# Fused cross attention and FFN in fp32: the transposes of the states' exponentials by block transposes and DMA, the sum of squares over blocks, and a new order of work

## Chip, cores and metric

The kernel runs on one core of a Trainium2 chip. The metric is the device time of one execution in microseconds. Three executions of the kernel before took 791.08, 791.44 and 792.14 us, median 791.44.

## What is computed

Attention of 8 batches, 8 heads, 512 tokens and 32 states of width 64: the tokens read the states, the states read the tokens, each with its own softmax over scaled scores. The result, 8 x (512 + 32) = 4352 rows of 512, goes through an RMS norm and a gated FFN of width 1536. Everything is fp32.

```python
scores  = x @ state.T / sqrt(64);  a  = softmax(scores);   xread = a  @ state
scores2 = state @ x.T / sqrt(64);  a2 = softmax(scores2);  sread = a2 @ x
rows = concat([xread, sread], axis=2)          # 4352 rows of 512
xn   = rows / sqrt(mean(rows ** 2) + 1e-6) * rms_g
out  = (silu(xn @ w_gate) * (xn @ w_val)) @ w_out
```

## The kernel before

**Stages.** At the start the weights are loaded and batch 0 is computed, beside the attention of batches 0 and 1 (string ORDER, one letter a step). Then the batches 1 to 7 follow, one period each; a period does batch b's FFN and, while b is under 7, the attention of batch b + 1. At the end the FFN of the 256 state rows of all batches is done together (string STATES).

**The FFN of a batch.** Since the token reads are a product of softmax weights and states, the gate and value weights are first multiplied with the batch's own states: `own_weights` (products at L528, copies at L539, both in the function at line 516). One call gives one of six pairs of column blocks, 16 matmuls on small 64x32 tiles of the array (a "group" in the profile is such a run of 16 passes). The hidden layer (`hidden_seven`, products at L674) and the projection (`project_seven`, products at L836) multiply 2x2 blocks with seven products instead of eight, the sums being kept in PSUM banks or formed by VectorE (DVE) and GpSimd (POOL). A product of the projection has two row halves r = 0 and 1, of 12 passes of 128x256 each; the two halves lie in one PSUM bank. When a bank holds a finished partial result, ScalarE (ACT) copies each half to SBUF (L873, names p1, p5, u2, c21), and the products that follow are summed on into the same bank: after p1 and p5 come the sums at L881, and u2 is copied after the product wt,hs, before wo,hb is added into the bank. SBUF sums of h (L888) and stores of the rows (L903, queue of SP) follow.

**The attention of batch b + 1** (`tokens_read` and `states_read`). For batches from 2 on, the scores come from small tiles (L346), in blocks of 32 tokens; DVE transposes blocks of 32x32 (L335, L403). The token reads are products on small tiles (L410), whose squares (ACT, L417) are added by DVE (L420). To get the mean square of each token, four matmuls with a column of ones (L424, eight passes in the profile: an fp32 product is two passes) sum over the partitions; DVE adds 1e-6 (L428), POOL takes the power (L270), four transposes against the identity on TensorE (PE; L277) spread the result over the partitions, and DVE multiplies the softmax weights with it (L434). For the state reads, ACT takes the exponentials of the states' scores (L452, scores copied at L360), PE transposes them, eight 128x128 blocks in two PSUM banks (L459), ACT copies these (L461), and products on small tiles (L471) multiply them with x. DVE divides by the sum (L463, L464, L478), PE transposes once more (L482), DVE copies the result to the state rows (L484).

**Order.** PE, DVE and ACT take their instructions in an order dealt by hand: each letter of PERIOD takes the next step of a generator. Letters h, t, u: products, copies, sums of the hidden layer; p, c, k: products, copies, sums of the projection; v, x: products and copies of own weights; a: `tokens_read(b + 1)`; s: `states_read(b + 1)`; w: the first own weights of batch b + 1. A step is what lies between two `yield`s. POOL and the DMA queues are placed by the framework, which also adds all waits, among them those between the two halves of a PSUM bank: a copy of one half waits for the products before it in the other half, and the products that follow in either half wait for it.

**Buffers.** PSUM pools: aps and vps (attention, own weights) of two banks each, fx of two, fy and fz of one each (FFN). `one` and `two` are SBUF pools of one and two buffers per name.

Of the kernel before, what the change touches and what calls it, by code (L numbers as in the profile page):

```python
# [8 lines left out]
F32 = mybir.dt.float32  # L9
# [3 lines left out]
ALU = mybir.AluOpType  # L13
ACTF = mybir.ActivationFunctionType
AXX = mybir.AxisListType.X
PSUM = bass.MemoryType.PSUM

P = 128
# [10 lines left out]
)  # L29

PERIOD = (
    "hhtvtvhtxhuxhuthhtuhuhtxhhhutuuuhthhuttxahhxhthuuuuuxhavuvhtxhtxhhttuauhxuxhxuut"
    "hhhtuhthutuuhuuuhhauuhtaaauxuhthautuuhhthuhuautaaphuuuapuaaaaacaasapcpaaaaaaaakp"
    "psackaauaacakkpapaakaacpsaskcsssppsasspwswkswxkxxkkpxpxccxss"
)

STATES = (
# [6 lines left out]
def kernel(  # L44
# [20 lines left out]
    nc = tc.nc  # L65
    VE, SE, GE, TE = nc.vector, nc.scalar, nc.gpsimd, nc.tensor
# [75 lines left out]
    GE.memset(bounds[:, 1:2], 255.0 * (1 << 23))  # L142
    rms_g = consts.tile([P, NI], F32, name="rms_g")


    w_d = [scratch.tile([P, NI, 2, 2, P], F32, name="w_d%d" % mp) for mp in range(NM // 2)]
    w_sb = {}
    wo = consts.tile([P, NM, DM], F32, name="wo")
    hb = consts.tile([P, NM, S], F32, name="hb")
# [117 lines left out]
    def mean_root(ss, n):  # L267

        ri = two.tile([P, NC], F32, name="ri")
        GE.tensor_tensor(out=ri[:, 0:n], in0=ss, in1=mhalf[:, 0:n], op=ALU.pow)  # L270
        return ri

    def along_rows(ri, n):

        rp = aps.tile([P, NC, P], F32, name="at")
        for c in range(n):
            TE.transpose(out=rp[:, c, :], in_=ri[:, c:c + 1].to_broadcast([P, P]), identity=ident)  # L277
        return rp.rearrange("p c t -> p (c t)")
# [4 lines left out]
    def scores(b, packed, soft):  # L283

        xb = x_sb[b]
        stT = two.tile([P, 4, Ns], F32, name="stT")
        tp = aps.tile([P, 4, Ns], F32, name="at")
        TE.transpose(out=tp.rearrange("p j n -> p (j n)"),
                     in_=packed.rearrange("p e d -> p (e d)"), identity=ident)
        yield  # L290
        VE.tensor_copy(stT, tp)
        yield "step"

        xT = one.tile([P, 4, NC, P], F32, name="xT", tag="xT")
        for c in range(NC):
            tp = aps.tile([P, 4, P], F32, name="at")
            for j in range(4):
                TE.transpose(out=tp[:, j, :], in_=xb[:, c, P * j:P * j + P], identity=ident)
            yield
            SE.copy(xT[:, :, c, :], tp)  # L300
            yield "step"


        sp = [aps.tile([P, S], F32, name="at") for e in range(2)]
        for j in range(4):
            for e in range(2):
                TE.matmul(out=sp[e][Ns * j:Ns * j + Ns, :], lhsT=stT[D * e:D * e + D, j, :],
                          rhs=xT[D * e:D * e + D, j].rearrange("p c t -> p (c t)"),
                          start=True, stop=True)
        yield  # L310


        sS = read[b] = two.tile([P, 2, NC, P], F32, name="sS")
        eS = soft["e"] = one.tile([P, 2, S // Ns, Ns], F32, name="eS", tag="eS")
        for e in range(2):
            VE.transpose(out=eS[:, e].rearrange("p k n -> p (k n)"), in_=sp[e])
            yield
            SE.copy(sS[:, e].rearrange("p c t -> p (c t)"), sp[e])
            yield "step" if e else None

        soft["st"] = stT
        soft["half"] = lambda e: eS[:, e]
        soft["back"] = lambda e: [(aT_s[b][:, e], eS[:, e].rearrange("p k n -> p (k n)"))]

    def scores_of_blocks(b, packed, soft):
# [30 lines left out]
        for g in (2, 3, 0, 1):  # L356
# [7 lines left out]
                                   eS[:, g].rearrange("p e c n -> p e (c n)"))  # L364
                                  for g in (2 * q, 2 * q + 1)]

    def tokens_read(b):
        packed, soft = rows.pop(b), {}
        yield from (scores if b < 2 else scores_of_blocks)(b, packed, soft)
        half = soft["half"]  # L370
        m1 = two.tile([P, 2, S // Ns], F32, name="m1")
        z1 = two.tile([P, 2, S // Ns], F32, name="z1")

        def along(t, e):
            return t[:, e].unsqueeze(2).to_broadcast([P, S // Ns, Ns])

        for e in range(2):
            VE.reduce_max(out=m1[:, e], in_=half(e), axis=AXX)
            yield
            VE.tensor_tensor(out=half(e), in0=half(e), in1=along(m1, e), op=ALU.subtract)  # L380
            yield
            SE.activation(out=half(e), in_=half(e), func=ACTF.Exp, scale=SCALE)
            yield "step"
        stT_g[b] = two.tile([P, 4, Ns], F32, name="stT_g")
        if b > 1:
            soft["st"] = aps.tile([P, 4, Ns], F32, name="at")
            TE.transpose(out=soft["st"].rearrange("p j n -> p (j n)"),
                         in_=packed.rearrange("p e d -> p (e d)"), identity=ident)
            yield
        VE.tensor_tensor(out=stT_g[b], in0=soft["st"], in1=rms_g.unsqueeze(2).to_broadcast([P, 4, Ns]),  # L390
                         op=ALU.mult)
        yield
        aT_s[b] = two.tile([P, 2, S], F32, name="aT_s")
        for e in range(2):
            VE.reduce_sum(out=z1[:, e], in_=half(e), axis=AXX)
            yield
            VE.tensor_scalar(z1[:, e], z1[:, e], 1e-9, None, op0=ALU.add)
            VE.reciprocal(z1[:, e], z1[:, e])
            yield
            VE.tensor_tensor(out=half(e), in0=half(e), in1=along(z1, e), op=ALU.mult)  # L400
            yield
            for to, blocks in soft["back"](e):
                VE.transpose(out=to, in_=blocks)  # L403
            yield "step"


        reads = [(aps, vps)[j // 2].tile([P, S], F32, name=("at", "pv")[j // 2]) for j in range(4)]
        for j in range(4):
            for e in range(2):
                TE.matmul(out=reads[j][D * e:D * e + D, :],  # L410
                          lhsT=packed[Ns * j:Ns * j + Ns, e, :],
                          rhs=aT_s[b][Ns * j:Ns * j + Ns, e],
                          start=True, stop=True)
        yield
        sq = one.tile([P, 4, S], F32, name="sq", tag="xT")
        for i, j in enumerate((2, 3, 0, 1)):
            SE.activation(out=sq[:, i, :], in_=reads[j], func=ACTF.Square, scale=DM ** -0.5)  # L417
            yield "step" if i == 3 else None
        for i, j in ((0, 1), (2, 3), (0, 2)):
            VE.tensor_tensor(out=sq[:, i, :], in0=sq[:, i, :], in1=sq[:, j, :], op=ALU.add)  # L420
            yield
        sp = aps.tile([P, NC], F32, name="at")
        for c in range(NC):
            TE.matmul(out=sp[:, c:c + 1], lhsT=sq[:, 0, P * c:P * c + P], rhs=ones,  # L424
                      start=True, stop=True)
        yield
        ss = two.tile([P, NC], F32, name="ss")
        VE.tensor_scalar(ss, sp, 1e-6, None, op0=ALU.add)  # L428
        yield "step"
        ri = mean_root(ss, NC)  # L430
        yield
        rp = along_rows(ri, NC)
        yield
        VE.tensor_tensor(out=aT_s[b], in0=aT_s[b],  # L434
                         in1=rp.unsqueeze(1).to_broadcast([P, 2, S]), op=ALU.mult)
        yield "step"

    def states_read(b):

        xb, sS = x_sb.pop(b), read.pop(b)  # L440
        e2 = one.tile([P, 2, NC, P], F32, name="e2")
        s2 = two.tile([P, 2], F32, name="s2")
        m2 = two.tile([P, 2], F32, name="m2")
        z2 = two.tile([P, 2], F32, name="z2")
# [4 lines left out]
        VE.tensor_scalar(s2, m2, -SCALE, None, op0=ALU.mult)  # L449
        yield  # L450
        for e in range(2):
            SE.activation(out=e2[:, e], in_=sS[:, e], func=ACTF.Exp, scale=SCALE,  # L452
                          bias=s2[:, e:e + 1], accum_out=z2[:, e:e + 1])
            yield "step" if e else None
        e2T = one.tile([P, 2, NC, P], F32, name="e2T")
        for e in range(2):
            tp = aps.tile([P, NC, P], F32, name="at")
            for c in range(NC):
                TE.transpose(out=tp[:, c, :], in_=e2[:, e, c, :], identity=ident)  # L459
            yield  # L460
            SE.copy(e2T[:, e], tp)  # L461
            yield "step"
        VE.tensor_scalar(z2, z2, 1e-9, None, op0=ALU.add)  # L463
        VE.reciprocal(z2, z2)  # L464
        yield
# [1 line left out]
        for e in range(2):  # L467
            for c in range(NC):
                for j in range(4):
                    h = 2 * j + e  # L470
                    TE.matmul(out=rp[Ns * j:Ns * j + Ns, e, :],  # L471
                              lhsT=e2T[:, e, c, Ns * j:Ns * j + Ns],
                              rhs=xb[:, c, D * h:D * h + D],
                              start=(c == 0), stop=(c == NC - 1))
        yield
# [567 lines left out]
```

## Time and profile before

| | |
|---|---|
| runs | 791.08, 791.44, 792.14 us |
| profiled execution | 791.18 us, its span 789.0 us |
| TensorE clock granted | 1.00 |
| ACT issues a DMA at L127 | two, at the start, 492 and 601 ns |
| POOL, first power (L270) | 32.94 us, idle for 30.54 us before |
| L403 DVE transpose 128x512 | 707 ns |
| L335 DVE transpose 128x1024 | 1235 ns |
| L395 DVE reduction 128x512 to 128x16 | 662 ns |
| L428 DVE add of 128x4 | 163 ns |
| L461 ACT copy of 128x512 | 580 ns, two a batch |
| L270 POOL power | 1737 ns |
| store of 128 KB / load of 512 KB / x_b, 64 KB / fours, 64 KB | 2.2 / 5.2 / 2.8 / 6.5 us from issue to landing |

The engines are PE, DVE, ACT and POOL; "PEld" is the loading of weights, which overlaps PE. The chain of waits follows the work that ended last back from the end, so that a piece of it is a time in which nothing else set the end. "PE at L424 x8" is eight passes that write the tile named "at". In a table of stretches, busy times stand by engine with the counts of instructions, then the TensorE clock granted, the share of the DMA engines' time that is busy, and the GB/s moved.

### The profile page before, as it was taken

Reading aid. Unit: us, or ns where it says so; the run is one execution under the profiler, and the core shown is the slowest. Engines: PE = TensorE matmul, PEld = TensorE weight load, DVE = VectorE, ACT = ScalarE, POOL = GpSimd, SP = SyncE. Lnnn points to the kernel's source line nnn. Section 1 sums busy time; section 2 is a strip of 40 time slices with the busy share of each in tenths; the row PEclk is TensorE's granted clock in tenths of the full one; section 3 lists DMA queues with packets and bytes.
Section 4 is the critical chain, followed back from the end, with each engine's and each line's share of the span. In section 5 each row is a group of like instructions: output and inputs, shape, how many; then the busy total and the mean of one; then the engine's idle time right before and its main releaser. Section 6 shows DMA issues by size and latency. Waiting matters only on the chain.

```text
span 789.0 us, 13559 instructions
## 1 busy us (share of the span) xinstructions
PE 776.5 (98%) x5478; PEld 603.5 (76%) x5478; DVE 521.5 (66%) x822; ACT 334.4 (42%) x560; POOL 170.9 (22%) x216
## 2 busy tenths in 40 slices
PE   6999999999999999999999999999999999999998
PEld 5643444788877887888878887788788887888996
DVE  4999997688338951897168833895189715781461
ACT  5998864552245323542255224532354225410320
POOL 0100003430244023410433024402341043400000
PEclk9999999999999999999999999999999999999999
DMA  9788865730075005610263008400530034201311
GB/s 286 226 287 298 276 191 167 217 122 1 25 239 181 2 18 181 227 22 17 102 206 121 1 26 257 163 2 15 201 154 7 14 106 149 108 7 34 121 54 27
DMA packets 69277, 95.77 MB, mean 121 GB/s; under 512 B 46432, under 2 KB 54112, under 8 KB 62304
## 3 DMA queue, kind: packets, MB, share of 16 engines
q1 hardware_dynamic: 67040, 94.33, 36.6%
q8 instruction: 43, 0.70, 0.4%
q10 hardware_dynamic: 2176, 0.59, 0.4%
q14 instruction: 18, 0.15, 0.1%
HBM read 79.69 MB, written 15.20 MB: 120 GB/s over the span
## 4 chain that ended last, share of the span: by engine, by line
PE 92%; DVE 5%; DMA 1%; issue 0%; ACT 0%; SPq 0%
PE f L674 37%; PE f L836 35%; PE f L776 5%; PE pv L570 4%; PE at L528 3%; PE pv L528 3%; DVE ex L248 1%; PE at L471 1%; PE at L410 1%; DVE raw L244 1%; PE at L346 1%; PE at L459 1%; PE at L424 1%; DMA raw<-in_moe_w_gate_dram 1%; DVE w_m L253 1%; PE pv L346 1%
## 5 line engine op out<-in xcount | busy, mean ns | idle before, releaser
L836 PE MATMUL f<-wo,hb 128*128 128x256 f32 x540 | 123.4, 380 | 0.2 <-ACT ot L873 0.2
L674 PE MATMUL f<-aT_s,v 128*128 128x256 f32 x504 | 120.6, 382 | 0.0
L836 PEld LDWEIGHTS f<-wo,hb 128*128 128x128 f32 x540 | 101.4, 190 | 13.6 <-ACT ot L873 0.4
L674 PEld LDWEIGHTS f<-aT_s,v 128*128 128x128 f32 x504 | 94.1, 190 | 19.6 <-DVE c L736 5.0
L736 DVE TENSOR_TENSOR g<-g,f 128x512 f32<-128x512 f32 (+1 forms) x96 | 61.8, 653 | 68.4 <-PE f L674 63.9
L674 PE MATMUL f<-aT_t,vs 128*128 128x256 f32 x336 | 87.1, 381 | 0.0
L270 POOL TENSOR_TENSOR ri<-ss,mhalf 128x4 f32<-128x4 f32 x8 | 13.5, 1692 | 320.4 <-DVE s L449 210.9
L727 ACT ACTIVATE hb<-g 128x1024 f32<-128x1024 f32 (+1 forms) x48 | 48.2, 1004 | 79.3 <-DVE g L736 79.3
L836 PE MATMUL f<-wt,hs 128*128 128x256 f32 x360 | 81.0, 381 | 0.0
L836 PEld LDWEIGHTS f<-wt,hs 128*128 128x128 f32 x360 | 67.3, 190 | 14.1 <-issue 5.1
L674 PEld LDWEIGHTS f<-aT_t,vs 128*128 128x128 f32 x336 | 63.2, 190 | 15.0 <-issue 5.9
L873 ACT COPY ot<-f 128x256 f32<-128x256 f32 x60 | 21.4, 373 | 123.0 <-PE f L836 123.0
L554 POOL TENSOR_TENSOR vs<-v 128x256 f32<-128x256 f32 x42 | 31.3, 746 | 164.2 <-ACT v L539 164.1
L739 DVE SCALAR_TENSOR_TENSOR hb<-hb,g 128x1024 f32<-128x1024 f32 x42 | 53.2, 1266 | 4.6 <-ACT hb L727 4.6
L725 ACT COPY g<-f 128x512 f32<-128x512 f32 (+1 forms) x48 | 26.9, 561 | 55.8 <-PE f L674 55.8
L776 PE MATMUL f<-wo,hb 128*128 128x512 f32 x96 | 44.7, 600 | 0.0
L557 POOL TENSOR_TENSOR vs<-v,vs 128x256 f32<-128x256 f32 x42 | 44.4, 1057 | 0.0
L570 PE MATMUL pv<-aT_s,v 128*128 128x512 f32 x96 | 43.7, 594 | 0.2 <-DVE aT_s L434 0.2
L674 PE MATMUL f<-aT_s,vs 128*128 128x256 f32 x168 | 43.1, 379 | 0.0
L674 PE MATMUL f<-aT_t,v 128*128 128x256 f32 x168 | 43.1, 379 | 0.0
L836 PE MATMUL f<-wo,hs 128*128 128x256 f32 x180 | 41.1, 379 | 0.0
L836 PEld LDWEIGHTS f<-wt,hb 128*128 128x128 f32 x180 | 33.7, 190 | 9.4 <-DVE ot L881 5.0
(144 smaller groups left out, 1277.0 us busy)
## 6 DMA issues: line engine op xcount, KB each, us to landing
w_m<-w_d SPq DMA_DIRECT2D x48, 1024.0 KB, 6.5
out_dram<-ot SPq DMA_DIRECT2D x56, 128.0 KB, 2.2
raw<-in_moe_w_val_dram SPq DMA_DIRECT2D x6, 1024.0 KB, 5.5
raw<-in_moe_w_out_dram SPq DMA_DIRECT2D x6, 1024.0 KB, 8.6
x_b<-in_x_dram SPq DMA_DIRECT2D x96, 64.0 KB, 2.8
w_d<-w_m SPq DMA_DIRECT2D x6, 1024.0 KB, 4.9
raw<-in_moe_w_gate_dram SPq DMA_DIRECT2D x5, 1024.0 KB, 7.1
x_b<-in_x_dram SPq DMA_DIRECT2D x6, 256.0 KB, 6.8
```

What stands on the lines that cost most here:

```text
L528: TE.matmul(out=pv[e][Ns * j:Ns * j + Ns, :], lhsT=stT_g[b][D * e:D * e + D, j, :], rhs=w[D * e:D * e + D, j].rearrange("p m k f -> p (m k ...
L554: GE.tensor_tensor(out=vs[:, 0], in0=a21, in1=a22, op=ALU.add)
L557: GE.tensor_tensor(out=vs[:, 2], in0=a12, in1=vs[:, 1], op=ALU.subtract)
L570: TE.matmul(out=to[0], lhsT=lhs(i, k), rhs=r, start=(i == 0), stop=(i == len(rhs) - 1))
L674: TE.matmul(out=ps[:, i, 0:half], lhsT=l[:, i, :], rhs=r, start=(start and i == 0 and k == 0), stop=(k == len(lhs) - 1), skip_group_check= ...
L725: SE.copy(gates(q)[1], q["x"][:, :, 0:half])
L727: SE.activation(out=hb[:, 2 * mp:2 * mp + 2, 0:n].rearrange("p m (c t) -> p m c t", c=2), in_=q["g"][:, :, :, 0:half], func=ACTF.Silu if s ...
L736: VE.tensor_tensor(out=to, in0=to, in1=q[ps][:, :, 0:half], op=ALU.add)
L739: VE.scalar_tensor_tensor(out=h, in0=h, scalar=1.0, op0=ALU.add, op1=ALU.mult, in1=q["g"].rearrange("p m c t -> p m (c t)"))
L776: TE.matmul(out=banks[r], lhsT=hb[:, m, P * r:P * r + P], rhs=wo[:, m, :], start=(m == 0), stop=(m == NM - 1))
L836: TE.matmul(out=banks[name][:, r, :], lhsT=lhs(k)[:, P * r:P * r + P], rhs=rhs(k), start=(start and r == 0 and k == 0), stop=(k == HM - 1) ...
L873: SE.copy(to, banks[name][:, r, :])
```

## The change

For batches 2 to 7 the exponentials of the states' scores are written by ACT in another layout (L493), transposed in 32x32 blocks by one DVE instruction (L512), written to DRAM by a DMA that ACT issues (L515, 512 KB), and read back in four DMAs of 128 KB each (L519), also issued by ACT. That replaces eight PE transposes and two ACT copies per batch. The small product L530 (old L471) takes its weights from the new layout.

For the same batches the sum of squares over the partitions is done by blocks (`rms_on_blocks`): DVE transposes 32x32 blocks (L395), sums each over its free axis (L398), one matmul with a fixed 128x128 matrix of 32x32 identities (`groups`, built by sixteen POOL operations at the start) adds the partition groups (L401, 128x128 by 128x16), and four DVE additions of 32 partitions each (L406) replace one of 128. `stT` moves from the pool `two` to `one`. Batches 0 and 1 keep the old way (`rms_on_array`).

The string PERIOD is dealt anew. ORDER and STATES stay as they are. In the new order the own weights' groups stand mostly alone between FFN products, and the two row halves of wo,hb in the projection (L896, old L836), with ACT's copy of the second half of u2 (L933, old L873) between them, follow one another on PE with nothing between. The lines of the old functions move down by 8 at first and by 38 to 60 from `tokens_read` on: L674 becomes L734, L836 L896, L528 L588, L410 L458, L277 L285, L420 L468, L881 L941, L888 L948.

```diff
--- before.py
+++ after.py
@@
 PERIOD = (
-    "hhtvtvhtxhuxhuthhtuhuhtxhhhutuuuhthhuttxahhxhthuuuuuxhavuvhtxhtxhhttuauhxuxhxuut"
-    "hhhtuhthutuuhuuuhhauuhtaaauxuhthautuuhhthuhuautaaphuuuapuaaaaacaasapcpaaaaaaaakp"
-    "psackaauaacakkpapaakaacpsaskcsssppsasspwswkswxkxxkkpxpxccxss"
+    "hhvttvhtxhuhuhxuxthuhtthuhhuthxhuxhuuhtthahuuthtuhuvhxutauhhtxutxhhuuhxhthvuuthh"
+    "axttxuhuuhthuhxhuuuutahhuahutthtuuhuahuuhupaatuauhauupucaaaasaaaaaaapsacksppsasc"
+    "aappacaacakpkakaupsaasaacaaspsakksaaaspkkpasawwsspxwxxckpxsxksxc"
 )
...
+    groups = consts.tile([P, 4, Ns], F32, name="groups")
+    for i in range(4):
+        GE.tensor_copy(groups[:, i], ident[:, 0:Ns])
+        for j in range(1, 4):
+            GE.tensor_tensor(out=groups[:, i], in0=groups[:, i],
+                             in1=ident[:, Ns * j:Ns * j + Ns], op=ALU.add)
...
+    e_d = [scratch.tile([4, Ns, 4, 8 * Ns], F32, name="e_d%d" % k) for k in range(2)]
...
+    def rms_on_array(b, sq):
...
+    def rms_on_blocks(b, sq):
+        n = S // Ns
+        VE.transpose(out=sq[:, 1, :], in_=sq[:, 0, :])
+        yield
+        part = one.tile([P, n], F32, name="part")
+        VE.reduce_sum(out=part, in_=sq[:, 1, :].rearrange("p (k f) -> p k f", f=Ns), axis=AXX)
+        yield
+        sp = aps.tile([P, n], F32, name="at")
+        TE.matmul(out=sp, lhsT=groups.rearrange("p i t -> p (i t)"), rhs=part,
+                  start=True, stop=True)
+        yield
+        ss = two.tile([P, NC], F32, name="ss")
+        for g in range(4):
+            VE.tensor_scalar(ss[Ns * g:Ns * g + Ns], sp[Ns * g:Ns * g + Ns, g::4], 1e-6, None,
+                             op0=ALU.add)
+        yield "step"
+        ri = mean_root(ss, NC)
+        yield
+        rp = along_rows(ri, NC)
+        yield
+        return rp
...
     def tokens_read(b):
...
-        sp = aps.tile([P, NC], F32, name="at")
-        for c in range(NC):
-            TE.matmul(out=sp[:, c:c + 1], lhsT=sq[:, 0, P * c:P * c + P], rhs=ones,
-                      start=True, stop=True)
-        yield
-        ss = two.tile([P, NC], F32, name="ss")
-        VE.tensor_scalar(ss, sp, 1e-6, None, op0=ALU.add)
-        yield "step"
-        ri = mean_root(ss, NC)
-        yield
-        rp = along_rows(ri, NC)
-        yield
+        rp = yield from (rms_on_array if b < 2 else rms_on_blocks)(b, sq)
...
     def states_read(b):
...
-        e2 = one.tile([P, 2, NC, P], F32, name="e2")
+        e2 = one.tile([P, 4, 2, NC, Ns], F32, name="e2")
...
         for e in range(2):
-            SE.activation(out=e2[:, e], in_=sS[:, e], func=ACTF.Exp, scale=SCALE,
+            to = e2[:, :, e].rearrange("p g c t -> p c g t")
+            if b < 2:
+                to = exps[:, e]
+            SE.activation(out=to, in_=sS[:, e].rearrange("p c (g t) -> p c g t", t=Ns)
+                          if b > 1 else sS[:, e], func=ACTF.Exp, scale=SCALE,
                           bias=s2[:, e:e + 1], accum_out=z2[:, e:e + 1])
...
-        for e in range(2):
-            tp = aps.tile([P, NC, P], F32, name="at")
-            for c in range(NC):
-                TE.transpose(out=tp[:, c, :], in_=e2[:, e, c, :], identity=ident)
-            yield
-            SE.copy(e2T[:, e], tp)
-            yield "step"
+        e2T = one.tile([P, 4, 2, NC, Ns], F32, name="e2T")
+        if b < 2:
...
+        else:
+            eB = one.tile([P, 4, 2, NC, Ns], F32, name="eB", tag="eS")
+            VE.transpose(out=eB.rearrange("p g e c n -> p (g e c n)"),
+                         in_=e2.rearrange("p g e c t -> p (g e c t)"))
+            yield
+            nc.scalar.dma_start(out=e_d[b % 2].rearrange("j t g f -> (j t) (g f)"),
+                                in_=eB.rearrange("p g e c n -> p (g e c n)"))
+            yield
+            for g in range(4):
+                nc.scalar.dma_start(out=e2T[Ns * g:Ns * g + Ns].rearrange("t j e c n -> t j (e c n)"),
+                                    in_=e_d[b % 2][:, :, g].rearrange("j t f -> t j f"))
+                yield
```

More of the change, by code (lines that the diff above doesn't have):

```diff
@@ L285, in scores @@
         xb = x_sb[b]
-        stT = two.tile([P, 4, Ns], F32, name="stT")
+        stT = one.tile([P, 4, Ns], F32, name="stT")
         tp = aps.tile([P, 4, Ns], F32, name="at")
@@ L365, in scores_of_blocks @@
                                   for g in (2 * q, 2 * q + 1)]
+    def rms_on_array(b, sq):
+        sp = aps.tile([P, NC], F32, name="at")
+        for c in range(NC):
+            TE.matmul(out=sp[:, c:c + 1], lhsT=sq[:, 0, P * c:P * c + P], rhs=ones,
+                      start=True, stop=True)
+        yield
+        ss = two.tile([P, NC], F32, name="ss")
+        VE.tensor_scalar(ss, sp, 1e-6, None, op0=ALU.add)
+        yield "step"
[13 more added lines that the diff above has]
+        TE.matmul(out=sp, lhsT=groups.rearrange("p i t -> p (i t)"), rhs=part,
+                  start=True, stop=True)
+        yield
+        ss = two.tile([P, NC], F32, name="ss")
+        for g in range(4):
+            VE.tensor_scalar(ss[Ns * g:Ns * g + Ns], sp[Ns * g:Ns * g + Ns, g::4], 1e-6, None,
+                             op0=ALU.add)
+        yield "step"
+        ri = mean_root(ss, NC)
+        yield
+        rp = along_rows(ri, NC)
+        yield
+        return rp
     def tokens_read(b):
@@ L440, in states_read @@
         xb, sS = x_sb.pop(b), read.pop(b)
-        e2 = one.tile([P, 2, NC, P], F32, name="e2")
+        e2 = one.tile([P, 4, 2, NC, Ns], F32, name="e2")
+        exps = e2.rearrange("p g e c t -> p (g e c t)").rearrange("p (e c s) -> p e c s", e=2, s=P)
         s2 = two.tile([P, 2], F32, name="s2")
@@ L451, in states_read @@
         for e in range(2):
-            SE.activation(out=e2[:, e], in_=sS[:, e], func=ACTF.Exp, scale=SCALE,
+            to = e2[:, :, e].rearrange("p g c t -> p c g t")
[3 more added lines that the diff above has]
+                          if b > 1 else sS[:, e], func=ACTF.Exp, scale=SCALE,
                           bias=s2[:, e:e + 1], accum_out=z2[:, e:e + 1])
             yield "step" if e else None
-        e2T = one.tile([P, 2, NC, P], F32, name="e2T")
-        for e in range(2):
-            tp = aps.tile([P, NC, P], F32, name="at")
-            for c in range(NC):
-                TE.transpose(out=tp[:, c, :], in_=e2[:, e, c, :], identity=ident)
-            yield
-            SE.copy(e2T[:, e], tp)
-            yield "step"
+        e2T = one.tile([P, 4, 2, NC, Ns], F32, name="e2T")
+        if b < 2:
+            flat = e2T.rearrange("p j e c n -> p (j e c n)").rearrange("p (e c s) -> p e c s", e=2, s=P)
+            for e in range(2):
+                tp = aps.tile([P, NC, P], F32, name="at")
+                for c in range(NC):
+                    TE.transpose(out=tp[:, c, :], in_=exps[:, e, c, :], identity=ident)
+                yield
+                SE.copy(flat[:, e], tp)
+                yield "step"
+        else:
+            eB = one.tile([P, 4, 2, NC, Ns], F32, name="eB", tag="eS")
+            VE.transpose(out=eB.rearrange("p g e c n -> p (g e c n)"),
+                         in_=e2.rearrange("p g e c t -> p (g e c t)"))
+            yield
+            nc.scalar.dma_start(out=e_d[b % 2].rearrange("j t g f -> (j t) (g f)"),
+                                in_=eB.rearrange("p g e c n -> p (g e c n)"))
+            yield
+            for g in range(4):
+                nc.scalar.dma_start(out=e2T[Ns * g:Ns * g + Ns].rearrange("t j e c n -> t j (e c n)"),
+                                    in_=e_d[b % 2][:, :, g].rearrange("j t f -> t j f"))
+                yield
         VE.tensor_scalar(z2, z2, 1e-9, None, op0=ALU.add)
@@ L471, in states_read @@
                     TE.matmul(out=rp[Ns * j:Ns * j + Ns, e, :],
-                              lhsT=e2T[:, e, c, Ns * j:Ns * j + Ns],
+                              lhsT=(e2T[:, j, e, c, :] if b > 1 else
+                                    flat[:, e, c, Ns * j:Ns * j + Ns]),
                               rhs=xb[:, c, D * h:D * h + D],
```

## The prediction

> **What bounds it.** I read first the busy shares, then the chain that ended last by engine:
>
> ```profile
> PE 776.5 (98%) x5478; PEld 603.5 (76%) x5478; DVE 521.5 (66%) x822; ACT 334.4 (42%) x560; POOL 170.9 (22%) x216
> ...
> PE 92%; DVE 5%; DMA 1%; issue 0%; ACT 0%; SPq 0%
> ```
>
> PE alone sets the time. In the chain the first products of batches 2 to 7 (pieces "L674 x8") begin at 223.04, 308.52, 394.00, 479.48, 564.96 and 650.43 us, 85.48 apart: six equal periods (batches 1 to 6, with batch b+1's attention inside), then batch 7's without attention and the states' rows. The changed work lies at a period's end; its chain:
>
> ```profile
> 287.55 0.79 PE at L424 x8
> 288.34 2.70 PE f L836 x12
> 291.04 0.44 PE at L277 x4
> 291.47 0.44 PE at L459 x4
> 291.91 5.18 PE f L836 x24
> 297.09 0.44 PE at L459 x4
> 297.53 2.59 PE f L836 x12
> 300.12 1.03 PE at L471 x64
> 301.15 1.02 PE pv L528 x16
> 302.17 0.86 PE at L528 x16
> 303.03 5.38 PE f L836 x24
> ```
>
> Nothing but PE, end to end: what PE no longer does is saved in full, every wait of PE costs in full, and other engines matter only where they come late. A 128x256 pass takes 5.18/24 = 0.216 us here. The group after L424 takes 2.70 instead of 2.59, and the one after the small tiles of L528 5.38 instead of 5.18: such pieces cost their neighbour too.
>
> **Part 1, off PE in each of six periods.** L424's eight passes: 0.79 + (2.70 - 2.59) = 0.90. L459's eight transposes: 2 x 0.44 = 0.88. Together 1.78.
>
> **Part 2, onto PE.** L401, one 128x128 by 128x16 product, two passes. No row has it; L424 (128x1) takes 0.90/8 = 0.11 a pass, a transpose (128x128) 0.11. I take 0.22; ends 0.11 and 0.38.
>
> **Part 3, the own weights' groups dealt apart.** The old order puts L528's groups in pairs or behind L471: five runs of small-tile work a period ({L528 x2}, {L528 x2}, L346, L410, {L471, L528 x2}). The new one has seven ({L588 x2}, L588, L588, L354, L458, {L588, L530}, L588). In batch 0 the chain shows both kinds:
>
> ```profile
> 99.95 1.02 PE at L528 x16
> 100.97 1.91 PE f L776 x4
> ...
> 109.75 1.72 PE f L776 x4
> ```
>
> A group alone costs 1.02 and makes the next full group 1.91 instead of 1.72, so about 1.21; the second of a pair costs 0.86. Each split adds 0.36 (ends 0.31 and 0.43, by the chain's 1.09 for another lone one): 0.72 a period. [...]
>
> **Part 4, waits for half a bank.** A copy of one half of a PSUM bank waits for the products already queued into the other half, and the products that refill its half wait for the copy. Before, this pair is covered:
>
> ```profile
> 291.07 0.37 ACT L873 COPY ot<-f 128x256 f32<-128x256 f32 x1 [1.55 <-PE f L836]
> 291.31 0.60 PE L459 MATMUL at<-ident,e 128*128 128x128 f32 x4
> 291.75 2.75 PE L836 MATMUL f<-wo,hb 128*128 128x256 f32 x12
> ```
>
> The copy starts as wo,hb's first half ends (291.04) and is done at 291.44, while PE does eight transposes to 291.91. In the new order wo,hb's second half (L896) follows the first directly on PE, and ACT's copy (L933) between them still waits for the first. The u2 copy of the other row lies beside the reads L458 (1.05 and the 0.2 behind it), one c21 copy beside a lone L588 (1.02): both longer than a copy with its ends (0.44). So one uncovered wait a period. It stands uncovered in the old kernel's last period, where no attention lies:
>
> ```profile
> 716.91 0.02 issue
> 716.93 0.38 ACT ot L873
> 717.31 0.04 issue
> 717.36 13.22 PE f L836 x60
> ```
>
> That is 0.44; 13.22 less 60 x 0.216 is 0.26 more for draining and restarting: 0.70. Ends 0.63 and 0.82. Behind the waiting product stand L401, wo,hs, L285 and all later PE work, so it is paid in full.
>
> **Part 5, DVE and ACT.** DVE gets the transposes L512 (128x1024, 1.24 by L335's row) and L395 (0.70, by L403's 707 ns for the same shape), the sum L398 (0.67, by L395 of the old kernel), and four 0.16 us adds instead of one: 3.1 us a period, beside 54.8 busy of 86. ACT loses two copies of 0.58 and gains five DMA issues (its old issues, at L127, took 0.49 to 0.60). What matters is lateness. Counting from the start of L458's products (0): squares end at 1.10 + 1.97 = 3.1. The three L468 adds, L395 and L398 end at 3.1 + 3 x 0.69 + 0.70 + 0.67 = 6.5 if L512 is done before the squares. L401 is due at 1.17 + 3 x 2.59 + 0.70 = 9.6: slack 3.1. Behind L401: four adds 0.64, POOL's power 1.74, so ri by 12.3; L285 is due at 9.64 + 0.22 + 5.18 = 15.0: slack 2.7. The DMA issue waits for L512, which follows exponentials before the reads; on ACT the bank copy of part 4 stands behind it, due at 1.17 + 2 x 2.59 = 6.4, so L512 has some 3 us. The rows for the window say there is room: columns are us, then busy of PE, PEld, DVE, ACT, POOL, clock, DMA share, GB/s.
>
> ```profile
> 281.00:288.00 7.00, 7.00 (x48) 5.51 (x47) 3.54 (x7) 2.70 (x6) 0.00 (x0) 1.00 0.16 47
> 287.00:297.00 10.00, 10.00 (x56) 8.92 (x55) 2.98 (x7) 2.75 (x7) 4.58 (x5) 1.00 0.04 15
> ```
>
> I cost all of it at nothing; one microsecond late is 6 us in all. [...]
>
> **Part 6, the round trip through DRAM.** The write (512 KB) and four reads (128 KB, 1 KB pieces) lie between eB and L530. L530 is due at 1.17 + 3 x 2.59 + 0.70 + 0.22 + 2 x 2.59 + 0.44 + 1.02 = 16.5, the write is issued by 3.1: 13.4, less 5 x 0.55 for issues, leaves 10.65 for both landings. By rows: a 512 KB load 5.2; 128 KB stores 2.2, and 64 KB loads in small pieces 2.8 (x_b) or 6.5 (fours). So 7.4 to 11.7; I take 5.2 + 2.8 = 8.0, hidden, DMA share being 0.04 there. Reads queue ahead of ACT's copies of the lone L588's bank, which come at 16.5: no loss.
>
> **Start and end.** POOL gets sixteen small operations at the start; its first power for a batch is 33 us in, and it idles before: nothing. In batch 7's period one more group is split (0.36) and one more copy stands almost uncovered (0.06): 0.42 added.
>
> **Sum.** Per period -1.78 + 0.22 + 0.72 + 0.70 = -0.14; six: -0.84; with 0.42: -0.4. The profiled execution took 791.18 (span 789.0 and 2.2 around it), 0.26 below the median of 791.44: 790.8 against it, 791.0 against the median. At all upper ends (+0.16 + 0.14 + 0.12 a period) it is +2.2: 793.6; at the lower ones, -2.2: 789.2.
>
> **Rivals.** (a) Faster, the bank wait isn't on the path: the framework's dependency may not tie the second half to that copy, or PE's queue hides it. Then six times -0.84, plus 0.42: -4.6, 786.8. For it: the six steady periods of before show no ACT piece; against it: the row at 716.91, and that there PE had other work in between.
> (b) Slower, the round trip is late. Place: L530 waits for the last read; price 6 us per us; it decides from 10.65 us for both landings. With the worst rows (5.2 + 6.5) it is 1.05 late: +6.3, 797.3. For it: 1 KB pieces, four reads on one queue behind one wait; against it: the idle DMA.
> (c) Slower, DVE's longer chain is late at L401 or the write's issue at the u2 copy: slack about 3, so it would take two 1.2 us operations queued ahead; 1 us late gives 797.
> (d) It doesn't do what it says: part 1's passes only stood where PE would have waited anyway. Part 4 has this already: 0.70 of 1.78.
>
> **Chances.** The sum 0.62 with its own range 789.2 to 793.6, of which 0.08 lies faster by over 0.2% (1.6 us, what a measurement here can tell from no change), 0.06 slower and 0.48 within. (a) 0.20, faster. (b) 0.10, (c) and the like 0.08, slower. Faster 0.28, same 0.48, slower 0.24. The range takes the sum and (a), 0.82: 786.6 to 793.6.
>
> **What will show it.** Periods 0.14 shorter (85.34). Right: an ACT piece of 0.38 at L933 between two L896 pieces in every period's chain; a lone L588 at 1.02 with its next group 0.2 longer; L401 about 0.2; no DMA or DVE piece near L530 and L401. Wrong: no ACT piece (a), "DMA e2T" before L530 (b), DVE before L401 or L512 before a late copy (c). A changed clock or POOL on the chain would be outside all of it.

## The result and the profile after

The changed kernel takes 791.60 us (median of 4 runs, 791.00 to 791.67), the kernel before 791.79 on the same chip: a ratio of 0.9997, 95% interval 0.9979 to 1.0014, no change that this measurement can tell. Forecast was a fall of 0.4. The changed kernel's profiled execution took 791.00, its span 789.2.

The page of the changed kernel, busy shares, then the chain by engine:

```profile
PE 774.4 (98%) x5394; PEld 593.0 (75%) x5394; DVE 545.2 (69%) x858; ACT 327.6 (42%) x548; POOL 173.8 (22%) x232
...
PE 94%; DVE 2%; ACT 2%; issue 0%; DMA 0%; SPq 0%
```

PE issues 84 passes fewer, DVE is busy 24 us longer (18.6, six times 3.1, were forecast), and PE is still the bound. In the chain the first products of batches 2 to 7 (pieces "L734 x8") begin at 223.31, 308.69, 394.07, 479.44, 564.83 and 650.20: a period of 85.38, against 85.48 before and 85.34 forecast. The end of such a period, in the changed kernel's chain (start, us, what):

```profile
285.39 5.39 PE f L896 x24
290.79 0.02 issue
290.81 0.38 ACT ot L933
291.19 0.04 issue
291.24 2.86 PE f L896 x12
294.09 0.13 PE at L401 x2
294.22 5.28 PE f L896 x24
299.50 0.44 PE at L285 x4
299.93 1.02 PE pv L588 x16
300.95 1.03 PE at L530 x64
301.98 2.79 PE f L896 x12
304.77 1.02 PE at L588 x16
305.79 2.79 PE f L896 x12
```

Every term of the sum can be read here. There are no passes with ones and no exponentials' transposes. ACT's copy stands on the path between wo,hb's halves: 0.44 of waiting, and a group of 2.86 instead of 2.59 behind it, 0.71 together. L401 takes 0.13, and the group behind it 5.28 instead of 5.18: 0.23. The last five rows hold the same products as the old rows from L471 to the 5.38 group, in 8.65 us (their sum) against 8.29: the second L588 stands alone and takes 1.02 instead of 0.86, and both groups of L896 now follow small tiles and take 2.79 instead of 2.59, where before only one paid this; 0.36 in all. The two DMA steps do not appear in the chain. Their rows:

```profile
e_d<-eB ACTq DMA_DIRECT2D x6, 512.0 KB, 2.9
e2T<-e_d ACTq DMA_DIRECT2D x24, 128.0 KB, 3.0
```

In the period shown eB is written from 285.67 on; the reads are issued from 290.89 to 292.65, since the first stands behind the copy of 290.81 on ACT; the last lands near 295.3. L530 begins at 300.95, so more than 5 us are left.

### The profile page after: what moved, and what is told of

Its sections match the earlier page's. It is cut to its first block, busy times and chain, and to the rows that moved or that the text cites. A ratio compares the mean times of both kernels' runs of the same rounds, so it can differ in the third digit from the quotient of the medians.

```text
span 789.2 us, 13508 instructions
## 1 busy us (share of the span) xinstructions
PE 774.4 (98%) x5394; PEld 593.0 (75%) x5394; DVE 545.2 (69%) x858; ACT 327.6 (42%) x548; POOL 173.8 (22%) x232
## 4 chain that ended last, share of the span: by engine, by line
PE 94%; DVE 2%; ACT 2%; issue 0%; DMA 0%; SPq 0%
PE f L734 38%; PE f L896 35%; PE f L836 5%; PE pv L630 4%; PE at L588 3%; PE pv L588 3%; PE at L530 1%; PE at L458 1%; PE at L354 1%; PE f L987 1%; PE pv L354 1%; PE at L285 0%; DMA rows<-in_state_dram 0%; PE at L306 0%; ACT ex L225 0%
## 5 line engine op out<-in xcount | busy, mean ns | idle before, releaser
L896 PE MATMUL f<-wo,hb 128*128 128x256 f32 x540 | 123.5, 381 | 3.0 <-ACT ot L933 3.0
L734 PE MATMUL f<-aT_s,v 128*128 128x256 f32 x504 | 122.5, 384 | 0.0
L896 PEld LDWEIGHTS f<-wo,hb 128*128 128x128 f32 x540 | 102.1, 190 | 18.9 <-ACT ot L933 5.6
L734 PEld LDWEIGHTS f<-aT_s,v 128*128 128x128 f32 x504 | 93.7, 190 | 24.9 <-issue 12.2
L734 PE MATMUL f<-aT_t,vs 128*128 128x256 f32 x336 | 87.1, 382 | 0.0
L933 ACT COPY ot<-f 128x256 f32<-128x256 f32 x60 | 21.3, 368 | 157.5 <-PE f L896 157.5
L896 PE MATMUL f<-wt,hs 128*128 128x256 f32 x360 | 82.2, 382 | 0.0
L278 POOL TENSOR_TENSOR ri<-ss,mhalf 128x4 f32<-128x4 f32 x8 | 9.3, 1157 | 330.5 <-DVE ss L406 223.8
L896 PEld LDWEIGHTS f<-wt,hs 128*128 128x128 f32 x360 | 67.3, 190 | 13.9 <-ACT ot L933 4.9
L734 PEld LDWEIGHTS f<-aT_t,vs 128*128 128x128 f32 x336 | 63.3, 190 | 14.8 <-issue 5.9
L599 ACT COPY v<-pv 128x512 f32<-128x512 f32 x42 | 23.7, 598 | 60.0 <-PE pv L588 60.0
L836 PE MATMUL f<-wo,hb 128*128 128x512 f32 x96 | 44.7, 600 | 0.0
L734 PE MATMUL f<-aT_t,v 128*128 128x256 f32 x168 | 43.1, 379 | 0.0
L734 PE MATMUL f<-aT_s,vs 128*128 128x256 f32 x168 | 43.1, 379 | 0.0
L896 PE MATMUL f<-wt,hb 128*128 128x256 f32 x180 | 42.6, 387 | 0.0
```

Of the source, the lines that this page charges most:

```text
L599: SE.copy(v[:, e].rearrange("p m k f -> p (m k f)"), pv[e])
L734: TE.matmul(out=ps[:, i, 0:half], lhsT=l[:, i, :], rhs=r, start=(start and i == 0 and k == 0), stop=(k == len(lhs) - 1), skip_group_check= ...
L836: TE.matmul(out=banks[r], lhsT=hb[:, m, P * r:P * r + P], rhs=wo[:, m, :], start=(m == 0), stop=(m == NM - 1))
L896: TE.matmul(out=banks[name][:, r, :], lhsT=lhs(k)[:, P * r:P * r + P], rhs=rhs(k), start=(start and r == 0 and k == 0), stop=(k == HM - 1) ...
```

## The experiments

A copy's wait is called covered where PE has other work while ACT copies. All kernels but one are the changed kernel with an edit; their periods are the distances between equal pieces in the chain of batches 1 to 6 (four or five of five agree within 0.02 us). The chain's place at the start of the first period differed from 139.2 to 140.4 us over the thirteen profiles of this study, whose opening part hardly differs, so sums are judged by periods, and medians beside them. Each ratio is to runs of the kernel before that were taken beside it (their medians are 791.79 to 791.91).

| kernel | period, us | median, us | ratio to before (95%) |
|---|---|---|---|
| before | 85.48 | 791.79 | |
| changed | 85.38 | 791.60 | 0.9997 (0.9979 to 1.0014) |
| e1_cover | 85.34 | 790.80 | 0.9985 (0.9976 to 0.9995) |
| e8_cover_hs | 84.77 | 787.11 | 0.9938 (0.9924 to 0.9953) |
| e2_pairs | 84.84 | 788.39 | 0.9957 (0.9942 to 0.9972) |
| e3_both | 84.81 | 786.65 | 0.9938 (0.9922 to 0.9955) |
| e9_all | 84.23 | 783.74 | 0.9901 (0.9886 to 0.9916) |
| e4_pe_exps_between | 85.52 | 792.32 | 1.0010 (1.0001 to 1.0019) |
| e5_array_rms_between | 85.32 | 791.46 | 0.9994 (0.9985 to 1.0004) |
| e6_before_blocks_rms | 85.32 | 790.54 | 0.9985 (0.9975 to 0.9994) |
| e10_all_array_rms | 84.79 | 786.43 | 0.9937 (0.9922 to 0.9952) |
| e11_all_pe_exps | 85.05 | 788.72 | 0.9960 (0.9946 to 0.9974) |
| e7_late_trip | 87.8 to 94.9 | 818.56 (one run) | |

**The copy's wait, covered: e1_cover.** The edit is in PERIOD alone, its last line: both u2 copies (c) and then the reads (a) follow wt,hs's second half (p).

```diff
-    "aappacaacakpkakaupsaasaacaaspsakksaaaspkkpasawwsspxwxxckpxsxksxc"
+    "aappacaakpccakakaupsaasaaaaspsakksaaaspkkpasawwsspxwxxckpxsxksxc"
```

> The changed kernel with one thing moved: the token reads (L458) stand behind both halves of wt,hs, and both u2 copies stand ahead of them, so that the copies lie beside the reads and wo,hb's second half waits for no copy. My theory (the uncovered wait costs 0.70 a period and is paid in full): a period of 85.38 becomes 84.68, and no ACT piece is left between two L896 pieces in the chain of batches 1 to 6; in batch 7's period, which has no reads, both copies stand uncovered together, 0.37 more; in all -3.8, about 787.8. Rival 1 (the wait only takes the place of another, such as L401 or L285 coming late, since the reads now begin 2.6 us later): the period stays near 85.4 and the time near 791.6, with DVE or POOL before L401 or L285. Rival 2 (only the 0.44 of the ACT piece is lost, the longer group behind it isn't part of it): a period of 84.94, about 789.4.

Measured: 85.34, only 0.04 less. The ACT piece is gone, and another engine stands in its place. Chain of e1_cover:

```profile
292.56 0.69 DVE part L398
293.24 0.88 DVE hs L948
294.12 0.04 issue
294.17 5.45 PE f L896 x24
```

So rival 1 held, though not at L401 or L285: DVE takes its work in the order dealt, and hs, which wo,hs needs, stood behind the squares' sums and the two new operations L395 and L398. Ahead of these the chain also holds ACT's squares, with the issue of the write (L515, 0.35) between them. What the change adds to DVE and ACT was free in the changed order, where PE waits for the copy; in this one it isn't. Batch 7's period became 0.4 shorter, where 0.37 longer was expected; my term for it was wrong, since the states' first products stand between there.

**The same with hs ahead: e8_cover_hs.** Two letters k (hs, L948) move ahead of the squares' sums.

```diff
-    "aappacaakpccakakaupsaasaaaaspsakksaaaspkkpasawwsspxwxxckpxsxksxc"
+    "aappacaakpccakakaupskkaasaaaaspsasaaaspkkpasawwsspxwxxckpxsxksxc"
```

> The kernel e1_cover with one more thing moved: the two subtractions hs (L948) stand on DVE ahead of the squares' sums, not behind the transpose and the sum over blocks (L395, L398). In e1_cover the copies were covered, but the chain went through the squares, L395, L398 and L948 to the product wo,hs, and gave a period of 85.34. Theory (the wait of 0.70 is real, and e1_cover only put DVE's longer queue in its place): with hs ahead the period is 84.68, 0.66 below e1_cover, and PE has no piece but its own between reads and L285; about 786.8. Rival (whatever is late is late for the squares themselves, which begin 2.6 us later: then L401 or L285 waits next): 84.9 to 85.3 with DVE or POOL pieces ahead of L401 or L285; 788 to 790.5.

Measured: 84.77, 0.61 under the changed kernel and 787.11. From the reads to L285 its chain holds PE alone, with one piece that is longer than before; that row of the chain, then the row of the timeline for its weights' load (in brackets the idle time before):

```profile
292.27 0.24 PE at L401 x2
```

```profile
292.12 0.30 PEld L401 LDWEIGHTS at<-part,groups 128*128 128x128 f32 x2 [0.25 <-issue]
```

L401 takes 0.24 instead of 0.13: L398 begins at 291.31 and lasts 0.69, so `part` is there at 292.00, and the load of L401's weights begins at 292.12, 0.15 before the 24 passes ahead of it end (292.27); in the changed kernel it begins at 293.71, 0.38 before that end. L401's new delay takes 0.11, so the covered wait gave 0.72. The price of 0.70 in the prediction is shown to be real and paid in full, once DVE is in time.

**The groups put together: e2_pairs.** One letter v moves next to another, and L530 stands ahead of both groups of the next batch.

```diff
-    "hhvttvhtxhuhuhxuxthuhtthuhhuthxhuxhuuhtthahuuthtuhuvhxutauhhtxutxhhuuhxhthvuuthh"
+    "hhvttvhtxhuhuhxuxthuhtthuhhuthxhuxhuuhtthahuuthtuhuvvhxutauhhtxutxhhuuhxhthuuthh"
...
-    "aappacaacakpkakaupsaasaacaaspsakksaaaspkkpasawwsspxwxxckpxsxksxc"
+    "aappacaacakpkakaupsaasaacaaspsakksaaaspkkpasawswswpxxxkpcxsxksxc"
```

> The changed kernel with the two groups of own weights that the new order splits off put back: L588 of the fourth and fifth pair of column blocks together, and L530 directly ahead of both groups of the next batch (with the c21 copy behind both halves of wt,hb, as in the kernel before). My theory (0.36 for each lone group): the period falls by 0.72 from 85.38 to 84.66, batch 7's period by 0.36; in all -4.7, about 786.9. Rival (the small tiles cost the same alone or in a pair, and the longer group behind a lone one is an effect of how ends are modelled): no change, 791.6.

Measured: 84.84, 0.54 less instead of 0.72; 788.39. Around L530 the rows give 8.29 instead of 8.65, all of the 0.36. In the hidden layer they give 30.08 instead of 30.27, only 0.19: the 60 passes behind the pair take 13.33, where its own last period, without attention, takes 13.15 for the same. The timeline of e2_pairs has the reason:

```profile
337.44 0.73 PEld L734 LDWEIGHTS f<-aT_t,v 128*128 128x128 f32 x4 [0.32 <-DVE c L796]
```

The lone group had stood just ahead of a product that waits for DVE to empty its bank. Half of its 0.36 was cover. The small tiles' price is real (the rival falls), and it too depends on what stands behind.

**Both at once: e3_both, then e9_all with hs ahead.** e3_both has the letters of e1_cover and e2_pairs, e9_all those of e8_cover_hs and e2_pairs.

> The edits of the two kernels before together: the copies of u2 covered by the reads, and no own weights' group split off. My theory (the terms add): the period falls by 1.42 to 83.96, batch 7's period gains 0.36 and loses 0.37; in all -8.5, about 783.1. Rival (with 1.4 us less of PE in a period something else comes late: the powers before L285, the copies of the own weights, or the return of the exponentials before L530): a period between 84.0 and 85.0 with DVE, POOL or DMA pieces in its chain, 784 to 789.

Measured: 84.81, with L398 and L948 of DVE in the chain as in e1_cover; the rival held. The groups took 0.53 off e1_cover's period, as they took 0.54 off the changed kernel's; what is missing is the covered wait, for the reason found in e1_cover.

> The three edits of e1_cover, e8_cover_hs and e2_pairs together: copies of u2 beside the reads, hs ahead of the squares' sums on DVE, no own weights' group split off. Theory (what was measured adds up: 0.61 for the covered wait with hs ahead, 0.54 for the groups): a period of 84.23, batch 7's period 0.4 shorter; about 783.6. Rival (e3_both gave only 84.81 because a period of this work cannot go under it, some other engine's round being the limit): 84.6 to 84.8, 785 to 786.7, with DVE, POOL or DMA pieces in the period's chain.

Measured: 84.23 and 783.74, as the terms add up. This is 1.0% under the kernel before (0.9901, 0.9886 to 0.9916), with nothing changed in the new code but the order.

**One part undone, at the place of the wait: e4_pe_exps_between, e5_array_rms_between.** Both take the old way for all batches; the old passes stand between wo,hb's halves. In e4_pe_exps_between (`states_read`; each test of b, and six letters s become four):

```diff
-    "aappacaacakpkakaupsaasaacaaspsakksaaaspkkpasawwsspxwxxckpxsxksxc"
+    "aappacaacakpkakaupaaaacsssaapsakkaaapkkpasawwsspxwxxckpxsxksxc"
...
-        if b < 2:
+        if b < B:
```

In e5_array_rms_between (`tokens_read`, and two letters a fewer):

```diff
-        rp = yield from (rms_on_array if b < 2 else rms_on_blocks)(b, sq)
+        rp = yield from (rms_on_array if b < B else rms_on_blocks)(b, sq)
```

> The changed kernel with the exponentials of the states' scores transposed on PE again for all batches (the way of batches 0 and 1, no DMA), the eight transposes put between the two halves of wo,hb, where ACT's copy is waited for. My theory: they cost 0.88 a period and hide the wait of 0.70, so the period grows by 0.18 to 85.56; in all +1.1, about 792.7, with no ACT piece in the chain. Rival 1 (the transposes cost their 0.88 wherever they stand, since the wait isn't on the path): 86.26, 796.9. Rival 2 (the round trip through DRAM holds the changed kernel up somewhere): the period falls below 85.38, the time below 791.

> The changed kernel with the mean square taken on PE again for all batches (eight passes with a column of ones, no L395 and L398), put between the two halves of wo,hb where ACT's copy is waited for. My theory: 0.90 comes back, 0.23 of L401 goes, and the wait of 0.70 is covered: the period falls by 0.03 to 85.35, 791.4, with no ACT piece in the chain of batches 1 to 6. Rival 1 (the wait is not what these passes cover): +0.67, 86.05, 795.6. Rival 2 (DVE's added work holds the changed kernel up where the chain doesn't show it): below 85.2.

Measured: 85.52 and 85.32, each within 0.04 of the theory and 0.7 from the first rival. Two rows of e4's chain tell it:

```profile
291.36 0.87 PE at L504 x8
292.23 2.59 PE f L896 x12
```

The eight transposes take 0.87, and behind them the group is 2.59 long again, with no ACT piece. Moving them to DVE and DMA saved 0.14 of 0.88 at this place, and taking the mean square off PE lost 0.06: each set free the same wait of 0.71.

**One part undone where nothing waits: e10_all_array_rms, e11_all_pe_exps.** The same two edits in e9_all's order.

> e9_all with the mean square on PE again for all batches (eight passes with the column of ones where L401 stood, no L395 and L398). Theory (where no copy is waited for, the eight passes cost PE all they take): 0.90 less 0.23 back, a period 0.67 above e9_all's, 84.90; 4.0 above it. Rival (these passes would be hidden again behind some other wait): within 0.2 of e9_all's period.

> e9_all with the exponentials of the states' scores transposed on PE again for all batches, four transposes behind L401 and four between the halves of wo,hs, no DMA. Theory (where no copy is waited for, eight transposes cost 0.88): a period 0.88 above e9_all's, 85.11; 5.3 above it. Rival (they cover something, as between the halves of wo,hb): within 0.3 of e9_all's period.

Measured: +0.56 and +0.82 a period, 786.43 and 788.72. The first is 0.90 less 0.34, because L401 costs 0.24 and 0.10 in e9_all; in the second the transposes take 0.48 and 0.44, and the 0.10 that L401 adds to its neighbour is gone, since they stand between. Here the saved passes are saved. No run has the old way of both in this order; if the two differences add, its period would be 85.61 (an estimate), no better than the 85.48 of the kernel before: the order would then pay only with the new code.

**The sum over blocks in the old order: e6_before_blocks_rms.** The kernel before with `rms_on_blocks` for batches 2 to 7 and two letters a more (L873 of its rows is L836 of before).

```diff
-    "psackaauaacakkpapaakaacpsaskcsssppsasspwswkswxkxxkkpxpxccxss"
+    "psackaauaacakkpapaaaakaacpsaskcsssppsasspwswkswxkxxkkpxpxccxss"
```

> The kernel before, in its own order, with the sum of squares over blocks alone (L395, L398, L401 in place of the eight passes; the exponentials' transposes stay on PE). My theory (the eight passes covered the copy of u2's first half): 0.79 and 0.11 go, the copy's 0.44 with the 0.27 behind it comes, L401 lies inside it; the period falls by 0.19 from 85.48 to 85.29, in all -1.1, about 790.7, with an ACT piece of 0.38 ahead of wo,hb in every period. Rival 1 (saved passes are saved): -0.67, 84.81, 787.8. Rival 2 (DVE's longer queue puts hs off ahead of wo,hs, as in e1_cover): above 85.4, 791 to 793, with DVE ahead of wo,hs.

Measured: 85.32 and 790.54, near the 85.29 and 790.7 of the theory and far from rival 1. But the chain names another engine:

```profile
287.67 0.70 DVE part L398
...
288.50 0.37 PE at L401 x2
```

L401's operands come at 288.37, and the copy of u2's first half runs from 288.38 to 288.75. Both are late by nearly the same time. The run shows that 0.5 of the saved 0.67 is lost at this place; which of the two would lose it alone, it doesn't tell.

**The round trip made late: e7_late_trip.** L512, the write and the reads move behind L406.

```diff
-    "aappacaacakpkakaupsaasaacaaspsakksaaaspkkpasawwsspxwxxckpxsxksxc"
+    "aappacaacakpkakaupaaaacaapakkaaasssssspkkpasawwsspxwxxckpxsxksxc"
```

> The changed kernel with the transpose of the states' exponentials (L512) moved behind the additions L406 on DVE, and write and reads behind it. By the rows of the changed kernel eB is then ready at 296.2 on the profile's clock, the write lands 2.9 later, the last of four reads is issued 1.3 later and lands 3.0 later: 303.4, while L530 is due at 300.95. My theory (the trip is hidden in the changed kernel by 5 us, and every us late is one in each of six periods): L530 waits 2.4 us for a DMA, a period of 87.8, in all +14.7, about 806. Rival (the trip overlaps whatever PE has queued, or the engine's queue runs ahead): 791.6.

Measured: 818.56, 27 us more instead of 14.7. The five distances between the first products of batches 2 to 7 are 94.9, 89.4, 89.2, 87.8 and 89.2. Chain in the second of them:

```profile
398.79 3.11 DMA e2T<-e_d
...
402.25 1.55 PE at L530 x64
403.80 3.96 PE f L896 x12
```

The lone L588 ends at 399.43, and L530 begins at 402.25. One product of 0.43 fits between, so 2.4 us are lost, as expected. The rest is the clock: it is at 0.50 from 402.7 to 406.1, so that L530 takes 1.55 instead of 1.03 and the next twelve passes 3.96 instead of 2.79, 1.7 more. The fourth distance shows the wait by itself: L530 begins at 580.82, as late as elsewhere, the clock stays at 1.00, and 87.8 is just 2.4 over the changed kernel. In the longest one the write takes 4.64 to land, and the weights' load of 1 MB is issued at 304.78, with the reads: the last of these takes 5.79, and the DMA engines are busy 0.78 of 306 to 312. The trip is hidden in the changed kernel because it is early, and it is not small.

## Why the prediction was right

**What bounds it** held: PE throughout, six equal periods.

**Parts 1 and 2** held. 0.90 and 0.88 a period leave PE (0.79 and 0.11 in e10_all_array_rms, 0.87 in e4_pe_exps_between); L401 is 0.23 against 0.22.

**Part 3** held: 0.36 and 0.37 for the two split groups. That 0.17 of one price is cover for a bank's wait was not in the prediction. The rows and e2_pairs fit 0.36 us for each separate run of small tiles; what in TensorE takes this time they do not show.

**Part 4** held to 0.01: 0.44 and 0.27 at the place named, and e8_cover_hs got 0.72 back. That the 0.27 goes to draining and restarting, as the prediction puts it, is not shown. Rival (a) is refuted by the ACT piece in the chain.

**Part 5** held for the changed kernel: L398 ends at 290.50 and L401 is due at 294.09, 3.6 us of room where 3.1 were counted. But "I cost all of it at nothing" is true of this order only; e1_cover and e3_both, where the copy's wait is covered, run into exactly these operations. The product that then waits is wo,hs, for hs behind L398 on DVE; the prediction looks at L401, L285 and the copy, and not at hs. The price given with it, 6 us in all for a microsecond late, holds only while the clock does: for 2.4 us of lateness the distances of e7_late_trip grew by 2.4 once, by 3.8 to 4.0 three times with a slower clock, and by 9.5 where the transfers landed later too.

**Part 6** held: 2.9 and 3.0 us for the landings, 5.9 where 8.0 was taken and 10.65 allowed. The 0.55 for an issue was 0.31 to 0.45. Between the landing of the write (near 288.6) and the first read's issue behind ACT's copy (290.89) some 2 us went by that were not counted; the room was large enough.

**The sum.** -1.78 + 0.23 + 0.73 + 0.71 = -0.11 a period from the rows, -0.10 measured, -0.14 forecast. Over six periods that is 0.6; batch 7's period with the rest took 139.0 instead of 138.6 us, 0.4 more, as forecast. Together -0.2, which is also the difference of the medians; but these cannot tell it from nothing (0.9979 to 1.0014 is -1.7 to +1.1 us), so it is the periods that bear the account. The profiled span is 0.2 longer, because its opening ended 0.36 later, within the scatter given above.

Rival (d) is in part what happened, and the prediction had priced it: of the 1.78 that PE saves in a period, 0.71 goes to the wait that the transposes had covered, 0.73 to the two split groups and 0.23 to L401. At the place of the wait either part undone changes the period by 0.14 or less (e4_pe_exps_between, e5_array_rms_between).

## What to carry to other kernels

Before taking work off a saturated engine, look for what is being waited for under it: short passes between two halves of a PSUM bank may be the only cover of a copy (0.71 us a period here). Price a removal at its own time less the wait it uncovers, and see what each engine has ahead of the next thing due in the order dealt (hs moved ahead took 0.57 off e1_cover's period); in this kernel three moves of order (copies beside the reads, hs ahead of the sums, groups in pairs) were worth 1.0% with the new code, which by itself gave nothing that could be measured. The transfer through DRAM was free here because it was issued early (more than 5 us were left; made late it held PE up for 2.4 us or more a period), so give such a transfer its lead first.

## What was not expected of the hardware

In e7_late_trip the granted clock fell to 0.50 around the late L530 in five of six periods, while the 0.44 of the copy's wait leaves it at 1.00 (from 287 to 297 in the changed kernel). In four of the five PE had stood still only twice, for 0.78 and for 1.05 to 1.27 us by the timeline, with a short product between; in the longest period these times are 2.54 and 3.43. From 402.73 on the clock is at 0.50 for 3.42 us; in the longest period it is so for some 10.2 (an estimate from the clock of its windows: 0.60 in 306 to 312, 0.50 in 312 to 316, 0.83 in 316 to 320). A stretch ahead of the fall at 402.73, the fall, then a stretch with the L530 at 580.82, where the clock did not fall (the columns are us, then busy of PE, PEld, DVE, ACT, POOL, clock, DMA share, GB/s):

```profile
399.32:402.73 3.41, 1.36 (x44) 0.81 (x39) 0.42 (x1) 1.07 (x2) 2.83 (x5) 1.00 0.96 287
402.73:406.15 3.42, 3.42 (x52) 2.79 (x41) 1.14 (x4) 0.00 (x0) 2.77 (x4) 0.50 0.56 197
580.00:584.00 4.00, 3.18 (x74) 2.89 (x75) 1.13 (x4) 0.00 (x0) 3.92 (x6) 1.00 0.70 273
```

PE stands still for nearly the same time at both places, 0.78 and 1.27 us ahead of the L530 at 402.25, 0.78 and 1.24 ahead of the one at 580.82, and at the other three falls of the four the second time is shorter still (1.19, 1.13 and 1.05). So the length of these gaps alone does not decide whether the clock falls, and what does is not shown. Nor is a limit in busy time: PE is busy for 1.36 us of the 3.41 ahead of the fall, but for 2.43 of 3.41 in the opening of the changed kernel (29.27 to 32.68), and there too the next 3.41 us run at 0.50.
